# Loads of the first batch's k and v, issued from two queues in place of one

## The chip, the cores and the metric

The kernel runs on one core of a Trainium2 chip. The metric is the device time of one execution in microseconds, and the median of several runs is compared. The engines are TensorE (PE, with its weight loads shown as PEld), VectorE (DVE), ScalarE (ACT), GpSimd (POOL) and SyncE (SP). Transfers are issued by an engine into its own queue (SPq, ACTq) and carried out by 16 DMA engines that all queues share.

## The reference

Attention over keys and values that are averaged over groups of eight positions, followed by a feed-forward layer, all in float32:

```python
# q, k, v: (8, 8, 576, 64); w_in: (512, 2048); w_out: (2048, 512)
k_p = k.reshape(B, H, 72, 8, D).mean(axis=3)
v_p = v.reshape(B, H, 72, 8, D).mean(axis=3)
attn = softmax(q @ k_p.T / 8)
x = (attn @ v_p).transpose(0, 2, 1, 3).reshape(4608, 512)
h = x @ w_in
out = maximum(0.01 * h, h) @ w_out
```

## The kernel before, in words

The feed-forward layer works on nine chunks of 512 tokens; its matrix products fill TensorE for most of the time. Attention of a batch is needed before the chunk that holds its tokens. At the start there is nothing to multiply: the first batch (batch 0) has to be loaded, pooled and put through attention by all engines together, then batch 1 likewise, and only then does the feed-forward stream begin. Weights arrive as 64-bit words and are converted to 32-bit parts by ScalarE (L204, L205, L216) and VectorE (L208 to L217) as the stream needs them.

The loads of batch 0 are written in `loads` (L784): k of heads 0 to 3 (tile k0raw, L280), the rest of k (kremraw, L314), the first queries (q, L462), k of heads 4 to 7 (k1raw), two more tiles of q, then v0raw, v1raw, the rest of v (vremraw, L323) and a fourth q tile. A raw tile holds 128 partitions of 2 x 512 numbers. `load_main` fills it in two transfers, partitions 0 to 63 with one head of each pair and partitions 64 to 127 with the other. A transfer of 64 partitions x 2 x 512 floats is 256 KiB in pieces of 2 KiB; a q tile is 256 KiB in pieces of 256 bytes. Behind batch 0 stand the k tiles of batch 1 (L295) and the first four pairs of weight blocks (L183, L187). All of these are issued by SyncE, one after the other, in this order.

Pooling adds eight neighbouring positions in three halving steps (`pooled`, L268 and L274). VectorE pools k, v1 and the rest of v (vremsum), GpSimd pools v0; v0 and v1 make up vsum. TensorE turns the key sums (pk, L496), ScalarE and VectorE scale them into kT_first (L498, L499), TensorE turns q (pq, L551) and makes scores (pss, L576), VectorE takes row maxima (red, L584), ScalarE exponentials (e, L588), VectorE or GpSimd normalise (at, L616 to L626), TensorE turns the result (pp, L682), and ScalarE copies it out (pT, L684 and L685). For the values ScalarE writes v_first (L521) from vsum and vremparts (L530) from vremsum, VectorE finishes vremparts (L532), and TensorE spreads them (pv, L540).

TensorE's order of instructions is written by hand (the string FIRST and what follows it). On the other engines a scheduler orders this opening when the program is built, from its own forecast of times, so their order can change when a load changes its queue. Within an engine instructions run in that order; each waits for what it reads.

Of the kernel before, what the change touches and what calls it, by code (L numbers as in the profile page):

```python
# [21 lines left out]
def tile_pooled_attention_ffn(  # L22
# [9 lines left out]
    nc = tc.nc  # L32
# [226 lines left out]
    def raw_tile(b, nm):  # L259
        shape = [P, 2, POOL * D]  # L260
        if (b, nm) in RAW:
            return spare(*RAW[b, nm], shape, F32, f"{nm}raw{b}")
        return two.tile(shape, F32, tag="raw", name=f"{nm}raw{b}")

    def pooled(eng, dst, raw, n, copies=1):
# [7 lines left out]
            a, b = (x.unsqueeze(2).broadcast_to(dst.shape) for x in (a, b))  # L273
        eng.tensor_tensor(dst, a, b, op=ALU.add)  # L274

    def load_main(b, src, g, nm):

        raw = raw_tile(b, f"{nm}{g}")
        for i in range(2):
            nc.sync.dma_start(  # L280
                raw[64 * i : 64 * i + 64, :, :],
                src[b, 4 * g + i : 4 * g + 4 : 2, : MAIN * POOL, :].rearrange(
                    "p (s a) d -> s p (a d)", a=POOL
                ),
            )
        return raw
# [33 lines left out]
    def load_v_rem(b):  # L320
        raw = raw_tile(b, "vrem")
        for w in range(2):
            nc.sync.dma_start(  # L323
                raw[64 * w : 64 * w + 64, 0, :],
                v[b, :, MAIN * POOL :, :].rearrange("h (s a) d -> h s (a d)", a=POOL),
            )
        return raw
# [31 lines left out]
    def load_v(b):  # L359

        sums = one.tile([P, NK, D], F32, tag="vsum", name=f"vsum{b}")
        rem = one.tile([P, 1, D], F32, tag="vremsum", name=f"vremsum{b}")
        raws = []

        def start():
            raws.extend(load_main(b, v, g, "v") for g in range(2))
            raws.append(load_v_rem(b))

        def finish():
            pooled(nc.vector if b == 1 else nc.gpsimd, sums[:, 0:2], raws[0], P)  # L370
            with issue_after(anchor["dve"].ins) if b == 0 else nullcontext():
                pooled(nc.vector, sums[:, 2:4], raws[1], P)
                pooled(nc.vector, rem, raws[2][:, 0:1, :], P)
            return sums, rem

        return start, finish

    def raw_steps(b):
# [3 lines left out]
        def load(n, keep=True):  # L382
            if n == 0:
                for g in range(2):
                    st["r", g] = load_main(b, k, g, "k")
                return
            if n == 2:
                if b > 2 and keep:
                    put_keys(st["ks"])
                st["r", 0] = load_main(b, v, 1, "v")  # L390
                st["r", 1] = load_v_rem(b)
                return
            if b == 2:
                st["r", 0] = load_k_rem(b)
                st["r", 1] = load_main(b, v, 0, "v")
                return
            st["r", 0] = raw_tile(b, "krem")
            for i in range(2):
                nc.sync.dma_start(
                    st["r", 0][32 * i : 32 * i + 32, 0, :],  # L400
                    k[b, i::2, MAIN * POOL :, :].rearrange("h (s a) d -> h s (a d)", a=POOL),
                )
            st["r", 1] = load_main(b, v, 0, "v")
# [1548 lines left out]
```

## Time and profile before

| | |
|---|---|
| median of 3 runs | 924.22 us (922.07 to 929.06) |
| the profiled execution's own time | 924.74 us |
| its span in the profile | 922.6 us |
| TensorE busy | 887.3 us, 96% of the span |
| VectorE busy | 496.9 us, 54% |
| ScalarE busy | 493.1 us, 54% |
| SyncE's queue (q1) | 150.55 MB, 59.8% of 16 engines' span |
| ScalarE's queue (q10) | 0.52 MB, 0.2% |

The times in the profile are from one execution, counted from the start of the span. A timeline row gives the start, the duration, the engine, the line of the kernel, the operation with output and input, the number of merged instructions, and in brackets how long the engine stood idle before it and what ended that. An issue on a queue is over when the transfer is handed over, not when the data have landed. Granted clock 1.00 is TensorE's upper level of 2.4 GHz, 0.50 the lower of 1.2 GHz.

### The profile page before, as it was taken

The numbers are of one execution on the slowest core, as the hardware profiler recorded it, in microseconds if no ns is written. First come the engines' busy times: TensorE is split into PE (matmuls) and PEld (weight loads), VectorE is DVE, ScalarE is ACT, GpSimd is POOL, SyncE is SP. The second block draws the span as 40 slices with busy tenths as digits, with TensorE's granted clock in tenths as the row PEclk, the third lists the DMA queues.
The fourth block names the chain that finished last, engine by engine and source line by source line (L and its number), as shares of the span: only waits on it lengthen the run. The fifth ranks groups of instructions, "written<-read, shape, count | busy, mean of one in ns | idle before, by whom it ended". The sixth has DMA issues, their size and how long they took to land.

```text
span 922.6 us, 15340 instructions
## 1 busy us (share of the span) xinstructions
PE 887.3 (96%) x5132; PEld 777.5 (84%) x5132; DVE 496.9 (54%) x1097; ACT 493.1 (53%) x1542; POOL 225.1 (24%) x374
## 2 busy tenths in 40 slices
PE   4887999999999999999999999999999999999998
PEld 3866788888888878989899988999989999999997
DVE  5799675624456765554835565545634643252222
ACT  4797765525355546655545655545645554353333
POOL 3011110144335835323702421222201110000000
PEclk9899999999999999999999999999999999999999
DMA  9996331234335697878876976575774564445442
GB/s 172 285 262 196 102 98 51 52 94 118 102 106 179 186 268 178 242 211 205 221 218 164 239 212 201 157 193 149 197 184 125 156 199 138 120 132 160 133 119 69
DMA packets 167254, 152.05 MB, mean 165 GB/s; under 512 B 114248, under 2 KB 131272, under 8 KB 167176
## 3 DMA queue, kind: packets, MB, share of 16 engines
q1 hardware_dynamic: 166600, 150.55, 59.8%
q8 instruction: 41, 0.67, 0.3%
q10 hardware_dynamic: 576, 0.52, 0.2%
q14 instruction: 37, 0.30, 0.1%
HBM read 120.21 MB, written 30.82 MB: 164 GB/s over the span
## 4 chain that ended last, share of the span: by engine, by line
PE 73%; DVE 8%; DMA 7%; ACT 4%; SPq 3%; issue 2%; POOL 2%; ACTq 0%; DVEq 0%; POOLq 0%
PE acc L1119 11%; PE acc L1120 11%; PE acc L1121 11%; PE pv L1235 4%; PE pv L1234 4%; PE pv L1233 4%; PE pu L1233 3%; PE pu L1235 3%; PE pu L1234 3%; PE pss L1489 2%; PE ph L1066 2%; PE ph L1068 2%; PE ph L1067 2%; SPq L280 1%; DMA k1raw<-in_k_dram 1%
## 5 line engine op out<-in xcount | busy, mean ns | idle before, releaser
L1119 PE MATMUL acc<-w,gh 128*128 128x512 f32 x576 | 232.7, 404 | 0.0
L1120 PE MATMUL acc<-w,gh 128*128 128x512 f32 x576 | 227.0, 394 | 0.0
L1121 PE MATMUL acc<-w,gl 128*128 128x512 f32 x576 | 225.3, 391 | 0.0
L1121 PEld LDWEIGHTS acc<-w,gl 128*128 128x128 f32 x576 | 108.5, 188 | 24.4
L1119 PEld LDWEIGHTS acc<-w,gh 128*128 128x128 f32 x576 | 109.3, 190 | 13.0
L1120 PEld LDWEIGHTS acc<-w,gh 128*128 128x128 f32 x576 | 109.3, 190 | 12.0
L616 POOL TENSOR_TENSOR at<-e,red 128x128 f32<-128x128 f32 x100 | 42.5, 447 | 231.8 <-DVE red L609 85.7
L1296 DVE TENSOR_TENSOR h<-held,pu 128x256 f32<-128x256 f32 x48 | 20.2, 420 | 118.8 <-ACT held L1295 118.8
L1233 PE MATMUL pv<-T,streamed 128*128 128x256 f32 x288 | 82.0, 285 | 0.0
L1234 PE MATMUL pv<-T,streamed 128*128 128x256 f32 x288 | 81.4, 283 | 0.0
L1235 PE MATMUL pv<-T,streamed 128*128 128x256 f32 x288 | 81.3, 282 | 0.0
L1261 DVE TENSOR_TENSOR gl<-h,gh 128x512 fp32r<-128x512 f32 x96 | 70.0, 729 | 10.6 <-ACT gh L1256 10.4
L1504 ACT ACTIVATE e<-pss,red 128x72 f32<-128x72 f32 x216 | 67.5, 325 | 11.5 <-DVE red L1497 5.5
L1295 ACT COPY held<-pv 128x256 f32<-128x256 f32 x48 | 17.9, 373 | 82.1 <-PE pv L1235 82.1
L1256 ACT CAST gh<-h 128x512 fp32r<-128x512 f32 x96 | 59.8, 623 | 1.6
L1233 PEld LDWEIGHTS pv<-T,streamed 128*128 128x128 f32 x288 | 54.5, 189 | 5.4 <-ACT held L1285 0.3
L1234 PEld LDWEIGHTS pv<-T,streamed 128*128 128x128 f32 x288 | 54.5, 189 | 5.1 <-DVE T L1748 0.3
L1307 DVE TENSOR_TENSOR held<-held,pu 128x256 f32<-128x256 f32 x48 | 20.2, 420 | 68.9 <-PE pu L1235 68.9
L1302 ACT ACTIVATE h<-pv 128x256 f32<-128x256 f32 x48 | 18.4, 384 | 67.9 <-PE pv L1235 67.9
L1235 PEld LDWEIGHTS pv<-T,streamed 128*128 128x128 f32 x288 | 54.6, 189 | 0.0
L1066 PE MATMUL ph<-x,w 128*128 128x512 f32 x128 | 52.2, 408 | 0.3 <-DVE gl L1076 0.3
L1068 PE MATMUL ph<-x,w 128*128 128x512 f32 x128 | 50.2, 392 | 0.5 <-DVE w L217 0.5
(248 smaller groups left out, 2146.8 us busy)
## 6 DMA issues: line engine op xcount, KB each, us to landing
streamed<-sums SPq DMA_DIRECT2D x120, 512.0 KB
w_bits<-in_moe_w_in_dram SPq DMA_DIRECT2D x16, 512.0 KB
w_bits<-in_moe_w_out_dram SPq DMA_DIRECT2D x16, 512.0 KB
sums<-sums SPq DMA_DIRECT2D x32, 256.0 KB
out_dram<-o SPq DMA_DIRECT2D x31, 256.0 KB
rows<-at SPq DMA_DIRECT2D x40, 192.0 KB
blocks<-rows SPq DMA_DIRECT2D x40, 120.0 KB
v0raw<-in_v_dram SPq DMA_DIRECT2D x16, 256.0 KB
```

Of the source, the lines that this page charges most:

```text
L616: eng.tensor_tensor(cols[:, :, i, :].rearrange("a (h w) y -> a h w y", h=2), e[:, 2 * i : 2 * i + 2, 0:MAIN].rearrange("a h (w y) -> a h w ...
L1066: nc.tensor.matmul(ph, w[:, 0, ks], xh[kk], start=kk == 0, stop=False)
L1068: nc.tensor.matmul(ph, w[:, 1, ks], xh[kk], start=False, stop=kk == NK - 1)
L1119: nc.tensor.matmul(a, gh[:, r], hi, start=first, stop=False)
L1120: nc.tensor.matmul(a, gh[:, r], lo, start=False, stop=False)
L1121: nc.tensor.matmul(a, gl[:, r], hi, start=False, stop=last)
L1233: nc.tensor.matmul(out, w[0][kk], x[:, 0, kk], start=start and kk == 0, stop=False, **args)
L1234: nc.tensor.matmul(out, w[0][kk], x[:, 1, kk], start=False, stop=False, **args)
L1235: nc.tensor.matmul(out, w[1][kk], x[:, 0, kk], start=False, stop=kk == 1, **args)
L1256: nc.scalar.copy(gh, h[:, i, :])
L1261: nc.vector.tensor_tensor(gl, h[:, i, :], gh.bitcast(F32), op=ALU.subtract)
L1504: nc.scalar.activation(st["e"][:, h, :], st["scv"][:, h, :], AF.Exp, bias=mx[:, h : h + 1], accum_out=sm[:, h : h + 1])
```

## The change

For batch 0 the second transfer of each raw tile of k and v, which fills partitions 64 to 127, is issued by ScalarE. The first one stays with SyncE, and so do q, krem, batch 1 and the weights. All other batches are loaded as before.

```diff
--- before.py
+++ after.py
@@ -273,11 +273,14 @@
             a, b = (x.unsqueeze(2).broadcast_to(dst.shape) for x in (a, b))
         eng.tensor_tensor(dst, a, b, op=ALU.add)
 
+    def queue_of(b, i):
+        return nc.scalar if b == 0 and i == 1 else nc.sync
+
     def load_main(b, src, g, nm):
 
         raw = raw_tile(b, f"{nm}{g}")
         for i in range(2):
-            nc.sync.dma_start(
+            queue_of(b, i).dma_start(
                 raw[64 * i : 64 * i + 64, :, :],
                 src[b, 4 * g + i : 4 * g + 4 : 2, : MAIN * POOL, :].rearrange(
                     "p (s a) d -> s p (a d)", a=POOL
@@ -320,7 +323,7 @@
     def load_v_rem(b):
         raw = raw_tile(b, "vrem")
         for w in range(2):
-            nc.sync.dma_start(
+            queue_of(b, w).dma_start(
                 raw[64 * w : 64 * w + 64, 0, :],
                 v[b, :, MAIN * POOL :, :].rearrange("h (s a) d -> h s (a d)", a=POOL),
             )
```

Three lines are added ahead of everything below, so later lines of the kernel carry numbers that are three higher. Five transfers go to ScalarE; SyncE's own ones keep their order among themselves.

The first place is ScalarE's start, before; raw tiles of batch 0 do not appear, and warm is a first exponential on one number.

```order
L157 ACT_TABLE_LOAD
L157 ACTIVATE warm<-warm 128x1
L498 ACTIVATE kT_first<-pk_0_220 64x2x64
L507 ACTIVATE kT_first<-pkr_225 64x4x8
L553 COPY qT_0_234<-pq_0_229 128x512
L498 ACTIVATE kT_first<-pk_2_249 64x2x64
```

And after:

```order
L283 DMA k0raw_161<-in_k_dram 64x2x512
L283 DMA k1raw_168<-in_k_dram 64x2x512
L283 DMA v0raw_175<-in_v_dram 64x2x512
L157 ACT_TABLE_LOAD
L157 ACTIVATE warm<-warm 128x1
L283 DMA v1raw_178<-in_v_dram 64x2x512
L326 DMA vremraw_181<-in_v_dram 64x1x512
L501 ACTIVATE kT_first<-pk_0_220 64x2x64
L510 ACTIVATE kT_first<-pkr_225 64x4x8
```

Three transfers now stand ahead of the table load and two behind the warm-up; then the first scaled keys follow as before, and a group of exponentials stands one place further ahead.

The second place is ScalarE between the last exponentials of the second q tile (e_1, red_1_1) and the pT copies of the first, before:

```order
L588 ACTIVATE e_1_274,red_1_1_301<-pss_1_1_298,red_1_1_301 128x72 x4
L588 ACTIVATE e_2_328,red_2_0_329<-pss_2_0_325,red_2_0_329 128x72 x4
L684 COPY pT_whole<-pp_0_0_351 128x2x128
L685 CAST pT_rem<-pp_0_0_351 128x128
L521 ACTIVATE v_first<-vsum_158 64x4x64 x2
L588 ACTIVATE e_2_328,red_2_1_345<-pss_2_1_342,red_2_1_345 128x72 x2
L530 ACTIVATE vremparts_337<-vremsum_159,own 128x64 x2
L588 ACTIVATE e_2_328,red_2_1_345<-pss_2_1_342,red_2_1_345 128x72 x2
L684 COPY pT_whole<-pp_1_0_358 128x2x128
```

And after:

```order
L591 ACTIVATE e_1_274,red_1_1_301<-pss_1_1_298,red_1_1_301 128x72 x4
L524 ACTIVATE v_first<-vsum_158 64x4x64 x2
L533 ACTIVATE vremparts_337<-vremsum_159,own 128x64 x2
L591 ACTIVATE e_2_328,red_2_0_329<-pss_2_0_325,red_2_0_329 128x72 x4
L591 ACTIVATE e_2_328,red_2_1_345<-pss_2_1_342,red_2_1_345 128x72 x4
L687 COPY pT_whole<-pp_0_0_351 128x2x128
L688 CAST pT_rem<-pp_0_0_351 128x128
L687 COPY pT_whole<-pp_1_0_358 128x2x128
```

v_first and vremparts have moved ahead of all eight exponentials of e_2, and the copy of pp_0_0 behind them.

The third place is VectorE where v1raw and vremraw are pooled, before:

```order
L268 TENSOR_TENSOR v1raw_178<-v1raw_178 128x2x256
L268 TENSOR_TENSOR vremraw_181<-vremraw_181 128x256
L608 TENSOR_TENSOR red_1_0_275<-red_1_0_275,tiny 128x4
L268 TENSOR_TENSOR v1raw_178<-v1raw_178 128x2x128
L584 TENSOR_REDUCE red_2_0_329<-pss_2_0_325 128x4
L268 TENSOR_TENSOR vremraw_181<-vremraw_181 128x128
L609 RECIPROCAL red_1_0_275<-red_1_0_275 128x4
L608 TENSOR_TENSOR red_1_1_301<-red_1_1_301,tiny 128x4
L274 TENSOR_TENSOR vsum_158<-v1raw_178 128x128
L584 TENSOR_REDUCE red_2_1_345<-pss_2_1_342 128x4
L274 TENSOR_TENSOR vremsum_159<-vremraw_181 128x64
L609 RECIPROCAL red_1_1_301<-red_1_1_301 128x4
```

And after:

```order
L268 TENSOR_TENSOR v1raw_178<-v1raw_178 128x2x256
L268 TENSOR_TENSOR vremraw_181<-vremraw_181 128x256
L611 TENSOR_TENSOR red_1_0_275<-red_1_0_275,tiny 128x4
L268 TENSOR_TENSOR v1raw_178<-v1raw_178 128x2x128
L268 TENSOR_TENSOR vremraw_181<-vremraw_181 128x128
L612 RECIPROCAL red_1_0_275<-red_1_0_275 128x4
L611 TENSOR_TENSOR red_1_1_301<-red_1_1_301,tiny 128x4
L274 TENSOR_TENSOR vsum_158<-v1raw_178 128x128
L274 TENSOR_TENSOR vremsum_159<-vremraw_181 128x64
L587 TENSOR_REDUCE red_2_0_329<-pss_2_0_325 128x4
L612 RECIPROCAL red_1_1_301<-red_1_1_301 128x4
L587 TENSOR_REDUCE red_2_1_345<-pss_2_1_342 128x4
```

The sums vsum and vremsum have moved ahead of the two row maxima on pss_2, which now follow them.

## Rows read from the trace of the kernel before

**Rows 1.** Busy time in three windows; columns in the first line.

```profile
core 0: us, PE busy (x) PEld busy (x) DVE busy (x) ACT busy (x) POOL busy (x), PEclk, DMA share, GB/s
20.00:25.00 5.00, 1.24 (x8) 0.66 (x7) 3.70 (x15) 2.83 (x16) 2.79 (x7) 0.95 0.82 164
25.00:30.00 5.00, 3.58 (x15) 3.43 (x16) 3.25 (x12) 3.66 (x17) 0.00 (x0) 0.50 0.97 267
50.00:60.00 10.00, 7.71 (x40) 5.80 (x39) 9.97 (x22) 10.00 (x32) 1.27 (x2) 1.00 1.13 301
```

**Rows 2.** TensorE's timeline, 0 to 60 us: start, us, engine, line, what, idle before.

```profile
8.58 1.06 PE L551 MATMUL pq<-ident,q 128*128 128x128 f32 x4
...
26.42 0.45 PE L540 MATMUL pv<-vremparts,spread 128*128 128x128 f32 x1 [2.43 <-DVE vremparts L532]
```

**Rows 3.** ScalarE's timeline, 0 to 60 us.

```profile
8.68 0.27 ACT L498 ACTIVATE kT_first<-pk 64x128 f32<-64x128 f32 x1 [5.36 <-PE pk L496]
...
22.29 0.32 ACT L588 ACTIVATE e<-pss,red 128x72 f32<-128x72 f32 x1 [2.15 <-DVE red L584]
...
23.49 0.38 ACT L684 COPY pT_whole<-pp 128x256 f32<-128x256 f32 x1
...
23.90 0.85 ACT L521 ACTIVATE v_first<-vsum 64x256 f32<-64x256 f32 x2
...
25.38 0.58 ACT L530 ACTIVATE vremparts<-vremsum,own 128x64 fp32r<-128x64 f32 x2
...
27.77 0.59 ACT L553 COPY qT<-pq 128x512 f32<-128x512 f32 x1 [0.79 <-PE pq L551]
28.41 0.37 ACT L684 COPY pT_hi<-pp 128x256 f32<-128x256 f32 x1
...
29.32 0.27 ACT L685 CAST pT_rem<-pp 128x128 fp32r<-128x128 f32 x1
...
35.38 0.73 ACT L204 ACTIVATE w_bits<-w_bits 128x512 f32<-128x512 f32 x1
```

**Rows 4.** VectorE's timeline, 0 to 60 us.

```profile
10.89 1.15 DVE L268 TENSOR_TENSOR k1raw<-k1raw 128x512 f32<-128x512 f32 x2 [1.50 <-DMA k1raw<-in_k_dram]
...
18.82 0.83 DVE L268 TENSOR_TENSOR v1raw<-v1raw 128x512 f32<-128x512 f32 x1 [0.21 <-DMA v1raw<-in_v_dram]
21.00 0.42 DVE L268 TENSOR_TENSOR vremraw<-vremraw 128x256 f32<-128x256 f32 x1 [1.35 <-DMA vremraw<-in_v_dram]
...
21.75 0.45 DVE L584 TENSOR_REDUCE red<-pss 128x4 f32<-128x288 f32 x1
...
23.02 0.30 DVE L274 TENSOR_TENSOR vremsum<-vremraw 128x64 f32<-128x64 f32 x1
```

**Rows 5.** Chain that ended last, 0 to 60 us: start, us, what.

```profile
12.55 8.35 DMA vremraw<-in_v_dram
```

**Rows 6.** SyncE's queue, timeline of its issues, 0 to 60 us.

```profile
0.74 1.44 SPq L280 DMA_DIRECT2D k0raw<-in_k_dram  x2
...
6.04 4.50 SPq L280 DMA_DIRECT2D v0raw<-in_v_dram  x2
...
11.87 1.29 SPq L323 DMA_DIRECT2D vremraw<-in_v_dram  x2
...
13.94 4.57 SPq L295 DMA_DIRECT2D k0raw<-in_k_dram  x2
...
25.36 0.56 SPq L183 DMA_DIRECT2D w_bits<-in_moe_w_in_dram  x1
```

**Rows 7.** DMA in windows 10 to 12, 12 to 16 and 30 to 35 us.

```profile
DMA packets 1466, 0.41 MB, mean 205 GB/s; under 512 B 1443, under 2 KB 1443, under 8 KB 1466
...
DMA packets 489, 0.84 MB, mean 209 GB/s; under 512 B 86, under 2 KB 86, under 8 KB 489
...
DMA packets 1266, 1.86 MB, mean 373 GB/s; under 512 B 60, under 2 KB 1065, under 8 KB 1265
```

**Rows 8.** ScalarE's timeline, 905 to 923 us: an issue from its queue.

```profile
917.82 0.34 ACTq L1432 DMA_DIRECT2D out_dram<-o  x1
```

## The prediction

> **What bounds the kernel now.** I read the windows first, then the chain that ended last in its opening 60 us, then each engine's timeline there. The reader is to see two things. Late in the opening, from 50 to 60 us, VectorE and ScalarE are busy 9.97 and 10.00 of 10 us [rows 1]: nothing waits there for the first batch any more, so a shift of these two engines is handed on to the end. Early, TensorE is busy only 1.24 of 5 us from 20 to 25 us and runs at the lower clock (granted 0.50) from 25 to 30 us [rows 1]. What starts it again is vector product pv at 26.42, after 2.43 us of waiting [rows 2]. Back from there: vremparts on ScalarE at 25.38, vremsum on VectorE at 23.02, and the first addition on vremraw at 21.00, which waited 1.35 us for its DMA [rows 3, 4]. The chain says the same: the last transfer of the first batch took 8.35 us from its issue at 12.55 to its landing near 20.9 [rows 5].
>
> Why so long? SyncE issues everything, and its issues themselves run into a full queue: two v0raw issues took 4.50 us, two k0raw issues of the next batch 4.57 us, where two first-batch ones at the start took 1.44 us [rows 6]. So the transfers behind are the limit, not the issuing. Their speed depends on the kind: 205 GB/s while mostly short pieces (under 512 B) of q move (10 to 12 us), 209 GB/s while mostly the 64-partition halves of v move (12 to 16 us), and 373 GB/s while the 128-partition weights move (30 to 35 us) [rows 7].
>
> **The change, part by part.**
> *Issues moved.* Five of SyncE's issues go to ScalarE: upper halves of k0, k1, v0, v1 (256 KiB each) and of vrem (128 KiB). On SyncE they cost 0.64 to 0.72 us each [rows 6] (1.29 and 1.44 for two), 3.4 us together, but that is hidden behind the full queue, where the same time is spent blocked; I take nothing for it. On ScalarE three stand ahead of the table load and two behind the warm-up. A ScalarE issue was seen only at the end of the kernel, 0.34 us [rows 8]; by the two rows five cost 1.7 to 3.6 us. The cover is the idle time of 5.36 us ahead of ScalarE's first copy, kT_first at 8.68 [rows 3]; so nothing is lost unless an issue is blocked as SyncE's were.
>
> *Transfers.* The first batch's k and v are eight halves of 0.262 MB, krem of 0.131 and two vrem of 0.131: 2.49 MB. At 209 GB/s that is 11.9 us, at the 373 GB/s of the full-width rows 6.7 us. So if lower and upper halves always moved side by side at full width, vremraw would land 5.2 us sooner; if the pair moved no faster than now, 0. Between them I work it out by what stands side by side. Only the k0 halves meet each other (0.524 MB: 2.5 us against 1.4, saves 1.1); ScalarE's other four transfers run beside SyncE's krem and q0, of which 0 to 1.9 us (krem 0.6 at 209 GB/s, q0 1.3 at 205) is hidden. At the end v0, v1 and vrem's lower halves are alone again. I take 1.1 plus half of 1.9: landing 2.0 us sooner, at 18.9 instead of 20.9.
>
> Here the trace and a rule point apart. Rows 7 show 209 GB/s for halves against 373 for whole width, which invites pairing them. The Trainium skill, SBUF — State Buffer, "Can I just issue two DMAs to hit both halves?", states that two concurrent DMAs on the two halves measured only 6% above one, because they serialize; the estimate by that page is 0.06 x 11.9 = 0.7 us for the landing, where the sum above has 2.0 us. No stretch of this trace has two queues on two halves, so neither is shown here.
>
> *Order of arrival.* The cost of the change is here. SyncE's lower half of k1 stands behind q0 as before, but ScalarE's queue need not wait for q0: the upper halves of v0, v1 and vrem (0.655 MB) can go ahead of k1's lower half. At 209 GB/s that is 3.1 us more ahead of k1; minus the same 1.1 and 0 to 1.9 us it is 0.1 to 2.0, and I take k1raw 1.1 us later (ends: 3.1 later with no overlap; 2.0 sooner if all that stands ahead of it, 1.83 MB, moved at 373 GB/s in 4.9 us with q0 hidden, against 6.9 us for k0, krem, q0 and k1 now). VectorE waits for k1raw at 10.89 already (1.50 us idle), and red and e follow from it, so all of this is paid: VectorE's first v1raw addition, at 18.82 for 0.83 us with only 0.21 us of idle time ahead of it, moves to 19.9, and vremraw starts at 19.65 + 1.1 = 20.75 instead of 21.00 [rows 4]. The DMA is then no longer what vremraw waits for; the exponentials' reductions are. Gain 0.25 us.
>
> *Order on VectorE and ScalarE.* The order now lets vsum and vremsum go ahead of the two reductions on pss_2 (one is 0.45 us at 21.75; successive rows overlap, so I count 0.36 for each), and v_first and vremparts ahead of the eight exponentials e_2. From the start of vremraw: vremsum ends at 23.32 - 21.00 - 0.72 = 1.6 us; v_first (0.85) has its vsum by about 1.35, one step ahead of vremsum, and ends at 2.2, vremparts at 2.8; eight exponentials (4 took 1.20 us, 22.29 to 23.49) end at 5.2; two pT pairs, one 0.41 us (23.49 to 23.90), at 6.0; qT_3 (0.59) at 6.6; two more pairs, about 0.7 us each from the spacing 28.41 to 29.59 halved upwards, at 8.0 [rows 3, 4]. Before it was 29.59 - 21.00 = 8.6 us. Gain 0.6 us. TensorE's pv comes some 2 us sooner than at 26.42, but TensorE then waits for these pT copies, which ScalarE does last: so the 0.6 counts, not the 2. ScalarE's weight conversion at 35.38 [rows 3] follows in the same order, and the weights have landed, issued from 25.36 on at up to 373 GB/s (1.05 MB in 2.8 us) [rows 6, 7].
>
> Sum: 0.25 + 0.6 = 0.85 us earlier. The profiled execution took 924.74 us (span 922.6, 2.1 around it), so 923.9 for it; it lies 0.5 us above the median of 924.22, on which I forecast 923.4.
>
> The lower clock from 25 to 30 us could also go, if TensorE's pause shrinks: 3.58 us busy there [rows 1] would be 1.8 us at the full clock. That is 0 to 1.8 us; TensorE waits for ScalarE there, so I take 0.
>
> **Rivals.**
> 1. *Slower: the halves serialize and only the order changes.* Place: VectorE's wait for k1raw. With no overlap k1raw lands 3.1 us later; vremraw starts at 19.65 + 3.1 = 22.75, 1.75 us later, minus 0.6: 1.15 us slower, 925.4. It decides as soon as k1raw is more than 1.95 us late. For it: the stretch at 205 to 209 GB/s has busy queues throughout [rows 7], so added bytes ahead cost time. Against it: short and long pieces leave one another gaps, if the engines are not full. The rule of the Trainium skill quoted above (same page and section) is this rival's case.
> 2. *Faster: full width.* All moves near 373 GB/s: k1raw 2.0 us sooner, vremraw at 17.65 or its landing at 15.7, whichever is later: 3.35 + 0.6 = 3.95 us, with the clock 5.75: 918.5 to 920.3, I say 919.4. For it: 373 GB/s exists on this chip in this kernel [rows 7]. Against it: the halves meet only at k0.
> 3. *The change doesn't do what it says:* ScalarE's issues are blocked by SyncE's full queue (3.86 us for one, the 4.50 of rows 6 less the 0.64 of another), so that the order of arrival stays; v1 and vrem issue no earlier than now and only the new order on the engines counts: 923.6. If the block lasts beyond 8.68 us, kT_first slips by about 1.2 us (6.04 + 3.86 = 9.9, less 8.68) and eats that again.
>
> **How the numbers follow.** Forecast 0.40 (923.4, its own range 921 to 926 with the scatter of medians); rival 1 0.28; rival 2 0.20; rival 3 0.12. The lowest case is 918.5, the highest 925.4 us; the three runs before spread from 922.07 to 929.06, so I add 1 us below and 2.5 us above: 917.5 to 928. One per cent, 9.2 us, is about what a measurement can tell from no change; no case reaches it, neither the 5.2 us of the landing with the clock's 1.8, nor 3.1 us of delay. Only what I have not seen does: 0.03 faster, 0.93 same, 0.04 slower.
>
> **What would show it right or wrong.** Right: VectorE's k1raw addition near 12.0 us; no DMA wait at vremraw, starting near 20.75; vremparts near 23 and ScalarE's first weight conversion near 34.5 us; SyncE's long blocked issues still there. q0 should be late too: TensorE's pq, at 8.58 now [rows 2], near or past 9.5. Wrong: k1raw at or before 10.9 (the pairing pays, rival 2) or past 12.9 (rival 1); a ScalarE issue of over 2 us (rival 3); DMA throughput between 3 and 16 us unchanged near 205 GB/s would refute the 2.0 us. If the first conversion moves but the end does not, the claim that 50 to 60 us hands on every shift is wrong.

## The result, and the profile after

The changed kernel takes 929.51 us in the median of 20 runs (927.0 to 938.65), the kernel before, run beside it, 924.26 us (921.05 to 929.91, 20 runs): a ratio of 1.006, 95% interval 1.004 to 1.008. It is 5.3 us slower, within one per cent as forecast, but 1.5 us above the predicted range. The profiled execution took 928.3 us with a span of 926.5, against 924.74 and 922.6 before.

The windows of the kernel after, the same three as in [rows 1] and two later ones (columns as there):

```profile
20.00:25.00 5.00, 3.23 (x20) 2.76 (x19) 4.27 (x14) 4.28 (x26) 3.72 (x6) 1.00 0.85 153
25.00:30.00 5.00, 2.73 (x16) 1.85 (x16) 3.95 (x16) 4.96 (x26) 1.54 (x4) 1.00 0.90 215
50.00:60.00 10.00, 7.73 (x39) 5.84 (x38) 9.96 (x22) 10.00 (x33) 1.27 (x2) 1.00 1.13 320
80.00:90.00 10.00, 7.18 (x35) 5.57 (x35) 9.54 (x20) 6.86 (x17) 2.42 (x2) 0.97 0.63 175
90.00:100.00 10.00, 10.00 (x47) 8.34 (x47) 4.23 (x12) 6.34 (x25) 1.94 (x4) 0.86 0.36 116
```

The two later windows of the kernel before:

```profile
80.00:90.00 10.00, 9.00 (x46) 7.03 (x47) 9.38 (x19) 7.20 (x17) 3.02 (x2) 1.00 0.63 189
90.00:100.00 10.00, 10.00 (x53) 8.46 (x51) 7.71 (x20) 9.15 (x37) 1.95 (x4) 1.00 0.36 106
```

From 20 to 30 us there is nothing bad to see: TensorE does more before 25 us, and the granted clock stays at 1.00 (2.4 GHz) where it was 0.50 (1.2 GHz). From 50 to 60 us all is as before. The loss stands between 80 and 100 us: TensorE is busy 7.18 us instead of 9.00, and then runs ten microseconds at a mean clock of 0.86 instead of 1.00.

TensorE's timeline after. The first two rows answer to [rows 2], the others lie where the loss is:

```profile
12.17 1.11 PE L554 MATMUL pq<-ident,q 128*128 128x128 f32 x4 [2.12 <-DMA q<-in_q_dram]
26.77 0.30 PE L543 MATMUL pv<-vremparts,spread 128*128 128x128 f32 x1 [0.77 <-DVE vremparts L535]
89.04 0.85 PE L554 MATMUL pq<-ident,q 128*128 128x128 f32 x4 [2.35 <-DVE x L733]
90.12 0.63 PE L1123 MATMUL acc<-w,gh 128*128 128x512 f32 x1
```

TensorE's timeline before, at that place:

```profile
86.63 0.60 PE L551 MATMUL pq<-ident,q 128*128 128x128 f32 x4
87.30 0.39 PE L1120 MATMUL acc<-w,gh 128*128 128x512 f32 x1
```

A transposition of q for batch 1 that before followed the products at once now waits 2.35 us for VectorE's x, and the product behind it takes 0.63 us instead of 0.39, at a granted clock of 0.50 (90 to 92 us).

ScalarE's timeline after, two of its issues, then the rows that answer to [rows 3], then x:

```profile
2.14 0.64 ACTq L283 DMA_DIRECT2D v0raw<-in_v_dram  x1
4.88 1.16 ACTq L326 DMA_DIRECT2D vremraw<-in_v_dram  x1
9.84 0.27 ACT L501 ACTIVATE kT_first<-pk 64x128 f32<-64x128 f32 x1 [5.53 <-PE pk L499]
24.75 0.84 ACT L524 ACTIVATE v_first<-vsum 64x256 f32<-64x256 f32 x2 [0.72 <-DVE vsum L274]
25.61 0.59 ACT L533 ACTIVATE vremparts<-vremsum,own 128x64 fp32r<-128x64 f32 x2
35.43 0.73 ACT L204 ACTIVATE w_bits<-w_bits 128x512 f32<-128x512 f32 x1
87.37 0.63 ACT L732 CAST x<-pa 128x256 fp32r<-128x256 f32 x2
```

VectorE's timeline after, answering to [rows 4], with k0raw ahead and x behind:

```profile
6.05 1.15 DVE L268 TENSOR_TENSOR k0raw<-k0raw 128x512 f32<-128x512 f32 x2 [1.66 <-DMA k0raw<-in_k_dram]
13.21 1.15 DVE L268 TENSOR_TENSOR k1raw<-k1raw 128x512 f32<-128x512 f32 x2 [2.67 <-DMA k1raw<-in_k_dram]
22.06 1.10 DVE L268 TENSOR_TENSOR v1raw<-v1raw 128x512 f32<-128x512 f32 x1
23.09 0.62 DVE L268 TENSOR_TENSOR vremraw<-vremraw 128x256 f32<-128x256 f32 x1
88.57 0.75 DVE L733 TENSOR_TENSOR x<-pa,x 128x256 fp32r<-128x256 f32 x2
```

Before, k0raw on VectorE, and x on ScalarE and on VectorE:

```profile
5.88 0.69 DVE L268 TENSOR_TENSOR k0raw<-k0raw 128x512 f32<-128x512 f32 x1 [1.48 <-DMA k0raw<-in_k_dram]
85.23 0.37 ACT L729 CAST x<-pa 128x256 fp32r<-128x256 f32 x1
85.63 0.42 DVE L730 TENSOR_TENSOR x<-pa,x 128x256 fp32r<-128x256 f32 x1
```

q0 is late by 3.6, k1raw by 2.3 and vremraw by 2.1 us, and yet the first weight conversion stands at 35.43 against 35.38: the opening is level again to 0.05 us. x (it is x_2 of batch 1) comes 2.9 us later on VectorE. TensorE's transposition writes the buffer of pa that x_2 is read from, so it must wait.

Part of what the opening gets back is the clock. TensorE's first and third group of products pa, before:

```profile
28.81 1.06 PE L710 MATMUL pa<-pT_whole,v_first 128*128 128x256 f32 x2
...
32.12 0.59 PE L710 MATMUL pa<-pT_hi,v_first 128*128 128x256 f32 x2
```

And after:

```profile
29.37 0.70 PE L713 MATMUL pa<-pT_whole,v_first 128*128 128x256 f32 x2 [1.18 <-ACT pT_whole L687]
...
32.03 0.59 PE L713 MATMUL pa<-pT_hi,v_first 128*128 128x256 f32 x2
```

Before, TensorE needs 3.31 us from the one to the other, never idle and at a granted clock of 0.50 up to 31 us. After, it needs 2.66 us at 1.00: 0.56 us late becomes 0.09 us early.

SyncE's queue after, beside [rows 6]:

```profile
5.96 2.52 SPq L465 DMA_DIRECT2D q<-in_q_dram  x2
8.53 5.21 SPq L283 DMA_DIRECT2D v0raw<-in_v_dram  x1
```

The chain that ended last, in place of [rows 5], now goes through q: issued at 2.36 us, it lands 9.77 us later.

```profile
2.36 9.77 DMA q<-in_q_dram
```

DMA after, from 2 to 5 us (with the rows of the two queues), 10 to 12 and 12 to 16 us, beside [rows 7]:

```profile
DMA packets 377, 0.71 MB, mean 236 GB/s; under 512 B 31, under 2 KB 31, under 8 KB 377
...
q10 hardware_dynamic: 234, 0.45, 59.1%
q1 hardware_dynamic: 143, 0.26, 31.8%
...
DMA packets 575, 0.37 MB, mean 185 GB/s; under 512 B 447, under 2 KB 447, under 8 KB 575
...
DMA packets 1868, 0.69 MB, mean 173 GB/s; under 512 B 1743, under 2 KB 1743, under 8 KB 1868
```

From 2 to 5 us in the kernel before:

```profile
DMA packets 451, 0.66 MB, mean 220 GB/s; under 512 B 142, under 2 KB 142, under 8 KB 451
```

From 2 to 5 us, with both queues at work on halves, the rate is 236 GB/s where it was 220, 7% more; but fewer packets are short (31 of 377 against 142 of 451), and other profiles scatter as much. In the seven with the changed kernel's transfers the rate is 206 to 236 GB/s there, in the eight with SyncE alone 198 to 220. From 12 to 16 us it is lower than before, 173 against 209, because q's short pieces have moved there. From 10 to 12 us it is lower too, 185 against 205, with fewer short pieces than before; why is open.

Why does x_2 come late? ScalarE's order in the program before, around it:

```order
L216 CAST w_7_966<-w_t_967 128x512
L1071 ACTIVATE ph_5_979<-ph_5_979 128x512
L729 CAST x_2_931<-pa_0_2_1004 128x256
L1074 CAST gh_5_1000<-ph_5_979 128x512
L204 ACTIVATE w_bits_708<-w_bits_708 128x512
L205 ACTIVATE w_bits_708<-w_bits_708 128x512
L204 ACTIVATE w_bits_885<-w_bits_885 128x512
L205 ACTIVATE w_bits_885<-w_bits_885 128x512
L729 CAST x_3_932<-pa_0_3_1009 128x256
```

And after:

```order
L1074 ACTIVATE ph_5_979<-ph_5_979 128x512
L216 CAST w_7_966<-w_t_967 128x512
L1077 CAST gh_5_1000<-ph_5_979 128x512
L204 ACTIVATE w_bits_708<-w_bits_708 128x512
L205 ACTIVATE w_bits_708<-w_bits_708 128x512
L204 ACTIVATE w_bits_885<-w_bits_885 128x512
L205 ACTIVATE w_bits_885<-w_bits_885 128x512
L732 CAST x_2_931<-pa_0_2_1004 128x256
L732 CAST x_3_932<-pa_0_3_1009 128x256
```

The scheduler has put two conversions of weights ahead of x_2, on VectorE likewise. From the first change in the forecast, at the loads, its order differs in places 80 us further on.

### The profile page after: what moved, and what is told of

The parts are those of the page before. It is cut to its first block, busy times and chain, and to the rows that moved or that the text cites. A ratio compares the mean times of both kernels' runs of the same rounds, so it can differ in the third digit from the quotient of the medians.

```text
span 926.5 us, 15339 instructions
## 1 busy us (share of the span) xinstructions
PE 887.4 (96%) x5132; PEld 776.2 (84%) x5132; DVE 497.8 (54%) x1097; ACT 492.8 (53%) x1542; POOL 224.5 (24%) x374
## 4 chain that ended last, share of the span: by engine, by line
PE 73%; DMA 7%; DVE 7%; ACT 4%; SPq 4%; issue 2%; POOL 2%; ACTq 0%; DVEq 0%; POOLq 0%
PE acc L1122 11%; PE acc L1123 11%; PE acc L1124 11%; PE pv L1238 4%; PE pv L1237 4%; PE pv L1236 4%; PE pu L1236 3%; PE pu L1238 3%; PE pu L1237 3%; PE pss L1492 2%; PE ph L1069 2%; PE ph L1071 2%; PE ph L1070 2%; DMA k1raw<-in_k_dram 1%; DMA blocks<-rows 1%
```

## The experiments

All kernels of the study do the same arithmetic. To tell the queue from the order, most of them have their order pinned: a dependency without a semaphore from each instruction to the next on GpSimd, ScalarE, VectorE and SyncE, over the opening and on to past 100 us. ORDER lists them by number, taken from the program before, the one after, or a piece of each; TensorE's order is the same in all. The kernel before with its own order pinned was not run; old_queue_open_new and old_queue_red_late, pinned and all on SyncE, stand at 1.000 (below), so pinning shows no cost of its own.

```diff
+def pinned(tc, nc, order):
+    made = {i.name: i for i in nc.cur_bb.bb.instructions}
+    for names in order:
+        row = [f"I-{n}" for n in names if f"I-{n}" in made]
+        for one, other in zip(row, row[1:]):
+            tc.add_manual_dep(made[other], one, mybir.DependencyInfo(
+                mybir.DependencyClass.NoSync, mybir.DependencyReason.DATA), reason="pinned")
...
-            by_hand.append(c)
+            pinned(tc, nc, ORDER); by_hand.append(c)
```

"Opening order" is what differs up to 35 us, "late order" what differs from 80 us on, together with SyncE's issues of batch 1's v and its rest, which change places near 40 us. In the tables the first conversion and the times of gl are starts in the profile, in us. gl (VectorE, L1076) is the low part of an activated block of the feed-forward layer; it is counted here as a marker, and where an expectation calls it a softmax step, that is wrong. The last column is from the 6th gl to the 7th. Medians and ratios are against the kernel before in the same rounds (medians 923.93, 923.63, 923.85 and 923.83 in the four sets). For comparison, the profiles of the kernel before and of the changed one:

| profile | first conversion | 5th gl | 11th gl | 6th to 7th |
|---|---|---|---|---|
| before | 35.38 | 76.04 | 125.19 | 9.34 |
| changed | 35.43 | 75.96 | 128.63 | 13.42 |

**Queue or order.** The queue move (the diff of the change, or not) and the two orders are crossed.

new_queue_late_old: 

> Five transfers on ScalarE's queue as in the changed kernel, and its order of instructions in the opening; only from batch 1's second half on (the stretch near 80 to 95 us) ScalarE, VectorE and SyncE stand in the order of the kernel before. Theory (the loss is the new place of x_2's cast and subtraction behind two weight conversions): TensorE's pq near 86.6 us starts without the 2.35 us wait, the granted clock stays 1.00 from 90 to 100 us, and the time is 923.5 to 925.5, about that of the kernel before. Rival (the transfers themselves cost the time, q0 and k1 being late): 928 to 930, as the changed kernel.

old_queue_late_new: 

> All transfers on SyncE as in the kernel before, with its opening order; only the late stretch stands in the changed kernel's order. Theory: the wait of some 2.3 us before pq and the lower clock behind it appear although no transfer was moved, 928 to 930. Rival: 923.5 to 925.

new_queue_old_order: 

> Five transfers on ScalarE's queue, all orders else those of the kernel before. Theory: the opening is late by what k1's and q0's landing cost without the new opening order: first weight conversion at 36 to 37.5 instead of 35.4 us, 925 to 926.5. Rival: 928 to 930. If the opening's delay were absorbed whatever the order, 924.3.

old_queue_new_order: 

> All transfers on SyncE, all orders else those of the changed kernel. Theory: the opening gains 0.5 to 2 us by its new order (first conversion at 33.5 to 35 us), the late stretch loses 3.5 to 5: 926.5 to 929. Rival: 924 or less.

| kernel | queues | opening | late | median, us | ratio (95%) | first conv. | 5th gl | 11th gl | 6th to 7th |
|---|---|---|---|---|---|---|---|---|---|
| new_queue_late_old | new | after | before | 927.10 | 1.0025 (1.0002 to 1.0048) | 36.23 | 77.16 | 126.83 | 9.33 |
| old_queue_late_new | old | before | after | 926.64 | 1.0021 (0.9994 to 1.0048) | 35.97 | 76.81 | 129.32 | 13.32 |
| new_queue_old_order | new | before | before | 925.74 | 1.0014 (0.9993 to 1.0035) | 36.57 | 77.28 | 126.40 | 9.35 |
| old_queue_new_order | old | after | after | 928.06 | 1.0034 (1.0010 to 1.0059) | 33.07 | 74.25 | 128.40 | 13.42 |

The last column sorts the kernels by their late order and by nothing else: 9.3 with that of before, 13.3 to 13.4 with that of after, whatever the queues do. The kernel with all transfers on SyncE and the orders of after is slower than the kernel before, although its first conversion comes 2.3 us sooner. So more than half of the loss (a ratio of 1.0034 against 1.006) needs no second queue, only the order that the second queue led the scheduler to. Two times missed what was expected. new_queue_late_old is at 927.10 instead of 923.5 to 925.5, although its pq has no wait: something is left that the late order does not make. old_queue_late_new has the wait (2.35 us) and the lower clock (0.83 from 90 to 100 us), but takes 926.64 us instead of 928 to 930, and its interval takes in no difference.

**Which piece of the late order.** Two kernels differ from the changed one and from the one before in x_2's cast and subtraction alone; the changed kernel ran beside them.

new_queue_x2_early: 

> The changed kernel with its queues and every order of its own except one: x_2's cast on ScalarE and its subtraction on VectorE stand again ahead of the two conversions of weights, as in the kernel before. Theory (these two places alone make the loss of 3.4 us between 80 and 125 us): x_2's subtraction under 86.5, the next transposition of q near 87 without a wait for VectorE, last gl 125 to 127, no granted clock under 0.95 between 90 and 100, the whole 2.5 to 4 us under the changed kernel run beside it. Rival (the other late swaps, or the later landing of weights, make it): last gl still near 128.5, no difference from the changed kernel.

old_queue_x2_late: 

> The kernel before, all on SyncE and every order its own, except that x_2's cast and subtraction stand behind the two conversions of weights as in the changed kernel. Theory: TensorE waits 2.2 to 3.3 us at the next transposition of q, which then starts near 89, last gl 128 to 129.5 against 125.2, the whole 2.5 to 4 us over the kernel before. Rival: last gl near 125.2 and no difference.

as_changed_again: 

> The changed kernel as it is, once more, so that it is measured in the same rounds as the two kernels that differ from it or from the kernel before in x_2's place alone: 927 to 930, ratio 1.003 to 1.007, last gl near 128.6.

| kernel | median, us | ratio (95%) | pq waits | 6th to 7th | 11th gl |
|---|---|---|---|---|---|
| as_changed_again | 929.43 | 1.0061 (1.0040 to 1.0082) | 2.98 | 13.13 | 130.03 |
| new_queue_x2_early | 927.30 | 1.0027 (1.0010 to 1.0045) | 0 | 11.07 | 126.85 |
| old_queue_x2_late | 927.95 | 1.0041 (1.0023 to 1.0059) | 2.87 | 13.15 | 130.16 |

TensorE and VectorE in old_queue_x2_late, and its windows:

```profile
90.74 0.99 PE L551 MATMUL pq<-ident,q 128*128 128x128 f32 x4 [2.87 <-DVE x L730]
...
90.27 0.74 DVE L730 TENSOR_TENSOR x<-pa,x 128x256 fp32r<-128x256 f32 x2
...
92.00:94.00 2.00, 2.00 (x6) 1.62 (x5) 0.69 (x1) 1.39 (x3) 0.00 (x0) 0.50 0.49 114
```

And in new_queue_x2_early:

```profile
86.82 0.60 PE L554 MATMUL pq<-ident,q 128*128 128x128 f32 x4
...
85.64 0.42 DVE L733 TENSOR_TENSOR x<-pa,x 128x256 fp32r<-128x256 f32 x1
...
92.00:94.00 2.00, 2.00 (x13) 1.63 (x12) 0.53 (x3) 1.32 (x8) 0.02 (x1) 1.00 1.10 303
```

Moved alone, x_2 makes the kernel before 0.41% slower, 3.8 us. In this trace the price has two parts: TensorE's pause of 2.87 us, and a granted clock of 0.50 behind it, at which 6 matmul rows lie in 2 us instead of 13. (The second part can turn up without the pause too, as the last section shows.) Put back in the changed kernel, x_2 returns 2.1 us (929.43 to 927.30), less than the 2.5 to 4 us expected, and the last gl is at 126.85: the stretch from the 6th to the 7th gl fell from 13.13 to 11.07 and not to 9.34.

The granted clock of every execution is on record, and by it the two comparisons differ. At 0.994, old_queue_x2_late took 927.0 us in the mean of seven executions and the kernel before, in the same rounds, 924.4 in thirteen: x_2 costs 2.6 us there at one clock. The changed kernel (as_changed_again) took 928.7 at 0.994 (five executions) and new_queue_x2_early 928.6 (two): at one clock no return is seen. What x_2 returned to the changed kernel goes with a higher clock, 0.9965 against 0.9932 in the mean of twelve executions each.

**What is left of that stretch.** In new_queue_x2_early VectorE takes the row maximum of pss_3_0 only behind the sum and reciprocal of red_2_1, which wait for ScalarE's exponentials.

new_queue_x2_red_early: 

> The changed kernel with x_2's cast and subtraction back ahead of the two conversions, and also the maximum over q_3's first scores (a reduction on VectorE) back ahead of the sum and reciprocal of q_2's second half. Theory (the second swap costs the 1.7 us between 86 and 97 us): the 7th softmax row step gl comes 9.3 to 9.7 us after the 6th instead of 11.07, last gl 125 to 125.6, the whole 924.5 to 926, 1 to 2 us under the 927.3 with x_2 alone put back. Rival (the new queues themselves cost what is left): last gl may move, the whole stays at 927 to 928.

old_queue_red_late: 

> The kernel before with one instruction in another place: the maximum over q_3's first scores stands behind the sum and reciprocal of q_2's second half. Theory: 6th to 7th gl 10.5 to 11.1 us instead of 9.34, last gl 126.2 to 127, the whole 1 to 2 us over the kernel before. Rival (the reduction's place is hidden): last gl near 125.2, no difference.

VectorE in old_queue_red_late, where this one instruction has moved:

```profile
91.52 0.45 DVE L584 TENSOR_REDUCE red<-pss 128x4 f32<-128x288 f32 x1
93.42 0.16 DVE L608 TENSOR_TENSOR red<-red,tiny 128x4 f32<-128x4 f32 x1 [0.85 <-ACT e L588]
...
93.71 0.44 DVE L584 TENSOR_REDUCE red<-pss 128x4 f32<-128x288 f32 x1
95.60 0.16 DVE L608 TENSOR_TENSOR red<-red,tiny 128x4 f32<-128x4 f32 x1 [1.45 <-ACT e L588]
```

The two maxima stand 2.19 us apart, where in the kernel before they start at 90.91 and 91.88. The stretch takes 10.30 us instead of 9.34, and with x_2 and this one put back in the changed kernel 10.10 instead of 11.07: in the traces it costs 1.0 us both ways (expected were 10.5 to 11.1 and 9.3 to 9.7). In the times it is not shown: old_queue_red_late 924.64 us, ratio 1.000 (0.998 to 1.002); new_queue_x2_red_early 925.90, ratio 1.0023 (1.0003 to 1.0043), 1.4 us under new_queue_x2_early with intervals that overlap. Its 11th gl, at 130.31, tells nothing of this: that profile lost 4.4 us to the clock before 60 us (last section).

**The queues by themselves.** Here the late order is that of before and the opening order that of after; only the place of the issues differs.

old_queue_open_new: 

> All ten transfers issued by SyncE as before; the opening's order of the compute engines is that of the changed kernel, the order from 80 us on (x_2's subtraction early) that of before. Theory (the new opening order is worth 1.8 us at 76 us as it was with the old queues and the late order, and the late order alone loses 3.4 us): first conversion of weights near 33, the 5th softmax row step gl near 74.2, the last gl near 123.4, the whole 1.8 us under before, near 922. Rival (whatever the opening gains is lost again before 125 us, as it was beside the late order, because the weights' transfers set the pace): last gl near 125, the whole near 924.

old_queue_open_new_again: 

> All on SyncE with the changed kernel's opening order and the late order of before, once more, since 1.3 us at 125 us in the trace stood against no difference in 12 runs. Theory (the gain is there and the scatter hid it): 921.5 to 923.5 where the kernel before has 924, ratio 0.997 to 0.999. Rival (the 1.3 us are within what profiles of one kernel differ by): ratio 0.999 to 1.002.

new_queue_late_old_again: 

> New queues, the changed kernel's opening order, all late orders of before, once more; old_queue_open_new differs from it in the queues alone and stood at 1.000 twice. Theory (the queues by themselves cost 1 to 3 us, since the first conversion came 2.5 us later than with SyncE alone): ratio 1.001 to 1.0035, first conversion 35.3 to 36.3. Rival (the 3 us of the first measurement were scatter): ratio 0.999 to 1.001, first conversion under 34.5.

| kernel | queues | median, us | ratio (95%) | first conv. | 5th gl | 11th gl |
|---|---|---|---|---|---|---|
| old_queue_open_new | old | 924.02 | 1.0002 (0.9973 to 1.0030) | 33.73 | 74.77 | 123.88 |
| old_queue_open_new_again | old | 924.18 | 0.9999 (0.9976 to 1.0022) | 33.66 | 75.09 | 124.75 |
| new_queue_late_old | new | 927.10 | 1.0025 (1.0002 to 1.0048) | 36.23 | 77.16 | 126.83 |
| new_queue_late_old_again | new | 925.29 | 1.0021 (0.9993 to 1.0049) | 36.29 | 81.65 | 130.80 |

With one order, the two queues make the first conversion 2.5 us later (36.2 to 36.3 against 33.7), and the kernel some 2 us slower; the second interval just takes in no difference. In the four profiles with the late order of the changed kernel or most of it the first conversion stands at 35.4 to 35.7, although the order up to there is the same; why is open. The new opening order is worth 1.7 us at the first conversion with SyncE alone (33.7 against 35.38; over all profiles with SyncE alone 33.07 to 33.73 in three against 35.20 to 36.31 in four). In the changed kernel the two cancel, by coincidence, which is why its opening looked unharmed. But of these 1.7 us only 1.3 and 0.4 are left at the 11th gl, and none in the times: the new opening order on the old queue neither beats the kernel before nor is beaten by it; the theory of 922 us fell twice.

**How the halves move.** In v_upper_late, k is wholly SyncE's, and ScalarE issues the upper halves of v behind its copy of qT_0, beside SyncE's lower halves. In k_upper_only and v_upper_only ScalarE issues at the start as in the changed kernel, but for one of the two inputs.

```diff
-            queue_of(b, i).dma_start(
+            queue_of(b, i * (nm[0] == "v")).dma_start(
```

For k_upper_only "k" stands there, and vrem stays on nc.sync.

v_upper_late: 

> k is issued wholly by SyncE; of v0, v1 and the v remainder the upper halves are issued by ScalarE, but only behind its copy of qT_0 (near 10 us), when k and q have landed, so that two queues carry the two halves of v at the same time with nothing else beside them. Opening order of the changed kernel, late order of before. Theory (two queues on two halves go only some 7% faster, as 236 against 220 GB/s between 2 and 5 us): pq_0 near 8.6 and k1raw near 11, as before; 10 to 16 us at 205 to 220 GB/s, vremraw between 19.5 and 21.5, the whole 921 to 924. Rival (a half moves at half width, two at full width): vremraw near 18, over 300 GB/s between 11 and 16 us, pv before 24, the whole under 921.

k_upper_only: 

> Only the upper halves of k0 and k1 are issued by ScalarE at the start; v and the v remainder stay with SyncE. Opening order of the changed kernel, late order of before. Theory (q's small pieces stand in SyncE's queue and share the DMA engines with whatever ScalarE's queue still holds; here that is 0.26 MB instead of 0.66): pq_0 between 9 and 10.5, k1raw 11 to 12, vremraw 20 to 21.5. Rival (the second queue itself, whatever it carries, delays q): pq_0 near 12, as in the changed kernel.

v_upper_only: 

> k is issued wholly by SyncE; the upper halves of v0, v1 and the v remainder are issued by ScalarE at the start, beside k. Opening order of the changed kernel, late order of before. Theory (bytes of v moved ahead of q take DMA time from k and q): pq_0 11 to 13, k1raw 13 to 15, the first k later than before's 6.49, vremraw 20 to 23. Rival (k's halves on two queues are what delays q): pq_0 near 8.6.

DMA in v_upper_late from 12 to 16 us, with both queues:

```profile
DMA packets 750, 0.82 MB, mean 205 GB/s; under 512 B 393, under 2 KB 393, under 8 KB 750
...
q1 hardware_dynamic: 606, 0.56, 74.7%
q10 hardware_dynamic: 144, 0.26, 32.1%
```

Two queues at work, 205 GB/s; the kernel before had 209 there with one [rows 7]. From 13 to 14.5 us, where only 18 of 154 packets are short, it is 186. Full width is refuted. What the theory missed is vremraw, at 24.13 us instead of 19.5 to 21.5, and not for its DMA: VectorE reached it late. ScalarE could issue vrem only at 15.64, and its first exponentials stand behind that issue:

```profile
16.86 0.32 ACT L591 ACTIVATE e<-pss,red 128x72 f32<-128x72 f32 x1 [6.17 <-DMA v0raw<-in_v_dram]
```

In old_queue_open_new and its repetition, with the same order and no issues on ScalarE, they start at 12.95 and 13.66. So ScalarE's waiting issues held up its own work by 3.2 to 3.9 us. The whole was 927.42 us (ratio 1.0029, 0.9999 to 1.0058), not 921 to 924.

q0 and k1raw in the other two, first k_upper_only (a single execution, 927.91 us):

```profile
9.94 1.12 PE L554 MATMUL pq<-ident,q 128*128 128x128 f32 x4 [0.34 <-DMA q<-in_q_dram]
```

and v_upper_only (a single execution, 930.09 us):

```profile
11.63 1.11 PE L554 MATMUL pq<-ident,q 128*128 128x128 f32 x4 [1.31 <-DMA q<-in_q_dram]
...
15.68 1.15 DVE L268 TENSOR_TENSOR k1raw<-k1raw 128x512 f32<-128x512 f32 x2 [4.86 <-DMA k1raw<-in_k_dram]
```

q0 is late by what has been put ahead of it: k1's upper half (0.26 MB, 1.25 us at 209 GB/s) delays TensorE's pq by 1.36 us, v's three upper halves (0.66 MB, 3.1 us) by 3.05. All together (0.92 MB, 4.4 us) delay it by 3.59; 0.10 MB of them moved only after 12 us. (pq waits for q0 in these kernels but not in the kernel before, so q0's own delay can be larger.) Bytes in a second queue cost the first queue about their full time here. So the theory holds for q0 in both kernels, while k1raw (expected 13 to 15) and vremraw (25.03, expected 20 to 23) came later still in v_upper_only: k has nothing from the second queue there and loses only.

## Why the prediction was wrong

The sum was 0.85 us faster; measured are 5.3 slower. By its steps:

- *Issues moved, cost nothing.* Right. ScalarE's issues took 0.62 to 1.16 us each and kT_first still waits for TensorE's pk (5.53 us). No issue of over 2 us, so rival 3 falls.
- *Transfers, landing 2.0 us sooner.* Wrong. The working took the full 1.1 us where the k0 halves meet and half of 1.9 us for hiding. Where they meet nothing was saved: VectorE waits for k0raw in both profiles and starts at 6.05 us instead of 5.88. The rates show 4.5% from 2 to 5 us in the means (220 GB/s in seven profiles, 210 in eight) and nothing from 12 to 16 us. The Trainium skill, SBUF — State Buffer, "Can I just issue two DMAs to hit both halves?", gives 6%. The traces agree with it within their scatter.
- *Order of arrival.* The mechanism was right and the size wrong: k1raw came 2.3 us later instead of 1.1, past the 12.9 us named as the mark of rival 1. q0's delay of 3.6 us was named ("near or past 9.5") and never priced. That vremraw starts without a wait for its DMA came out, but at 23.09 and not 20.75: VectorE reached it late.
- *Order on VectorE and ScalarE, 0.6 us.* About right at the row that it was worked out for: from the start of vremraw to the end of the fourth pT pair the changed kernel took 7.8 us (23.09 to 30.85), the kernel before 8.6. With the later arrival that row came 1.26 us late, where rival 1 had 1.15 slower and the forecast 0.85 faster. At the first conversion the order is worth more: with SyncE alone it comes 1.7 to 2.3 us forward. That the changed kernel is level at 35 us is later arrival, order and clock cancelling by chance.
- *The clock, taken as 0.* The lower clock from 25 to 30 us did go. "TensorE waits for ScalarE there" holds up to the first pa and not behind it: in the kernel before TensorE was never idle from there to the third pa, and the upper clock gained 0.65 us. No gain is left in the times, and the lower clock appeared elsewhere, as the last section shows.
- *"From 50 to 60 us a shift is handed on to the end."* The step's own test refutes it for the times: on the old queue the first conversion moved 1.7 us in two profiles, the median of 12 runs not at all, twice. Up to the 5th gl the traces do hand on a shift of 1.0 and 1.3 us; behind that 1.3 and 0.4 are left at the 11th gl. Where the rest goes is not shown.
- *What was left out: the order from 80 us on.* This is the step that failed. "Order on VectorE and ScalarE" was read down to 35 us, the weight conversion "follows in the same order", and all behind it was taken to be equal but shifted, at a price of nothing. The order of the changed program, which can be read before any run, has x_2 behind two conversions, with TensorE's next transposition waiting for x_2's buffer. Shown: alone it costs 3.8 us on the kernel before, and taking it back returns 2.1 of the 5.6 us that the changed kernel lost in those rounds. The sum has no term for the queues' own cost of some 2 us either; rival 1's mechanism, bytes ahead of q0 and k1, was seen in the opening.

In that set and the next the 5.6 us go as follows: 2.1 to x_2 (with a higher clock, as above), 1.4 to the row maximum (1.0 in the trace; in the times not told from 0), and 2.1 remain for new_queue_x2_red_early, as much as the two queues cost by themselves with the late order of before (3.2 and 1.5 us over the kernel before). Where in the kernel these last 2 us are paid is open: the profile of the changed kernel stands level with the one before at the first conversion and at the 5th gl, and the profiles of one kernel differ by more than that.

No version beat the kernel before.

## What to carry to other kernels

Where a scheduler orders the program at build time, a small change in what it forecasts moves instructions far away from the edit; compare the whole order of both programs, and ask of every instruction that moved back whose buffer it frees. DMA engines that are already full got no faster here with a second queue: the bytes put there delayed what the first queue wanted sooner, and in one kernel the engine that issued them too. And a lower clock in one stretch of one profile is not a saving to be counted on: here it went from there, others appeared elsewhere, and the medians show no gain.

## What the hardware showed that was not expected

The lower clock does not keep to one place. With the opening order of before, all five profiles have 0.50 to 0.66 from 25 to 30 us. With that of after, ten of twelve have 1.00 there, but all of those ten except new_queue_x2_early have ten microseconds at a mean of 0.87 or less later, at different places up to 100 us, in some of them behind x_2's pause and in others without it. Three of the five with the opening order of before have such a stretch too (0.83, in old_queue_late_new, old_queue_x2_late and old_queue_red_late), so it is not shown that the later ones take the place of the early one. Two profiles are at 0.51 to 0.52 from 40 to 50 us, although TensorE is never idle in it and no order of the computing engines differs there from that of the changed kernel, whose clock was 1.00. One of the two, new_queue_late_old_again, where TensorE's last pause before it ended at 31.14 us:

```profile
40.00:50.00 10.00, 10.00 (x40) 9.14 (x40) 5.82 (x12) 5.97 (x16) 0.00 (x0) 0.51 0.96 208
```

40 matmul rows in it, 58 in the kernel before; the 5th gl comes at 81.65, against 77.16 in the first profile of the same kernel. Over whole executions the clock does go with the time. In the four sets the kernel before has 47 executions at a granted clock of 0.994 with a mean of 923.9 us, 25 at 0.996 with 922.9, and 6 at 0.990 with 927.2. Its 122 times correlate with the clock at -0.72. The changed kernel took 929.1 us in its six executions at 0.994. So much of the scatter within one kernel is the clock, but the loss of the changed kernel is not a lower mean clock.
